# A fused linear attention with two feed-forward layers on one core: the plain slots' sine put ahead of the copies, and the preparation sums set out anew

## The chip, the core and the metric

The kernel runs on one core of a Trainium2 chip. The core has five engines with a queue each: TensorE (PE; its weight loads are PEld), VectorE (DVE), ScalarE (ACT), GpSimd (POOL) and SyncE (SP, which here only issues DMAs). Each engine takes its own instructions in the order in which the program issues them; between engines only semaphores set the order. The metric is the time of one execution on the device in microseconds (us).

## The reference

A recurrent attention over 768 time steps, then two layers of two matrix products each, with a rational function and then h·cos(h) between them. The work that the change touches lies in the last layer.

```python
def _attn_ref(q, k, v, alpha):            # B, H, S, D = 4, 8, 768, 48
    for t in range(S):
        state = alpha[:, :, t, :, None] * state + einsum('bhd,bhe->bhde', k[:, :, t], v[:, :, t])
        y[:, :, t] = einsum('bhd,bhde->bhe', q[:, :, t], state)
def _moe_ref(x, w_in, w_out, a, b):       # x: 3072 x 384, w_in: 384 x 2048, w_out: 2048 x 384
    h = x @ w_in
    P = a[0] + a[1] * h + a[2] * h**2 + a[3] * h**3
    Q = 1.0 + abs(b[0]) * abs(h) + abs(b[1]) * h**2
    return (P / (Q + 1e-06)) @ w_out
def _moe2_ref(x, w_in, w_out):            # same shapes
    h = x @ w_in
    return (h * cos(h)) @ w_out
```

## The kernel before

The 3072 tokens are six blocks of 512. The 2048 inner columns of a layer are 16 tiles of 128 (f = 0 to 15). Every fp32 operand is held as two parts, hi (rounded to the matmul's fp32r) and lo (the remainder), and a product is three matmuls (hi·hi, lo·hi, hi·lo), so a first product h = x·w_in of a tile is 9 matmuls of 512 columns and a second product (into three PSUM accumulators acc0 to acc2) another 9.

A **layer slot** (`layers(n)`) does one tile: a first product for tile n (L504), the activation of older tiles on ACT and DVE (the product g on DVE L599), the rounding of g to hi (ACT L550) and its remainder lo (POOL L555), and the second product of tile n-4 (L520). Blocks 0 and 1 of the last layer run this way. In block 0 DVE, ACT and POOL also convert the output weights (ACT L68, L69 and L188, DVE L73 and L74, POOL L198: the remainder of a weight tile that TensorE's second product needs a slot later), and round x for block 1 (ACT L630, DVE L634).

Blocks 2 to 5 of the last layer run in **plain slots** (`threes(k)`, k = 0 to 68; slot 0 is the first). There a 3 x 3 group of w_in tiles is multiplied with 15 half-width first products instead of 18 (a fast 3 x 3 scheme on sums and differences of the weights and of x). Three slots make one group (kinds 0, 1 and 2), five groups make 15 of the 16 tiles, and a slot of kind 3 (k = 15, 31, 47, 63) does the sixteenth tile by an ordinary first product of 9 matmuls (L1107). I call the slots 15, 31 and 47 **border slots**: they also run the first three products of the next block (`level0`), and ACT copies these from PSUM into s5 and s63 (L1025). Each plain slot does the activation of one tile: z (ACT L1003), the angle (DVE L1007), the sine (ACT L1011) and the product g = sine·h (DVE L1016); a slot later ACT rounds g to hi (L1021) and POOL forms lo (L1022); a slot after that TensorE does the second product (L965). DVE combines the partial products of a group in PSUM (L1049, L1058, L1066 to L1068, L1077, L1078); TensorE may write a bank again only when DVE has read it.

The sums and differences themselves are made beforehand by jobs: `weights()` for the five groups of w_in tiles (t = 0 to 4; `w_first` and `w_second`), `x_prepare(blk)` for x. A job is a generator. After every slot from layer slot -16 on (the counter `now`; plain slot k is now = 16 + k), `prepare(dve, pool, act)` adds a slot's budget to each engine's `room`; it first issues the pending remainders (POOL L654), then the pending roundings (ACT L651), and then lets each job issue sums (L660, on DVE or POOL as the job says) as long as **both** DVE and POOL have room left. The budgets are `EARLY` in the layer slots of block 0 (`now` below 0), `PLAIN` in those of block 1, and `ROOM[kind]` in the plain slots.

The banks: h of the sixteenth tile goes to bank b2, which the last tile of group 4 (its h is f1, also b2) holds until its product g (L1016) has read it. In a border slot the queue of ACT is z, hi, the two copies, sine; that of DVE is angle, g.

The last four tiles of block 1 still need their second products when the plain slots begin: slots 0 to 3 do 9 matmuls each of these (`old` in L990 to L994); slot 4 has none, and from slot 5 on the second products of block 2 follow.

Of the kernel before, what the change touches and what calls it, by code (L numbers as in the profile page):

```python
# [20 lines left out]
NF = DFF // 128  # L21
# [18 lines left out]
def attn_then_two_moe(ctx, tc, kqT, aT, vP, w1i, w1o, ma, mb, w2i, w2o, out):  # L40
# [601 lines left out]
    split = set()  # L642
# [5 lines left out]
    def splits(keys, hi, lo, of, cols):  # L648

        def first():  # L650
            nc.scalar.activation(out=hi, in_=of, func=AF.Copy)  # L651

        def rest():
            nc.gpsimd.tensor_tensor(out=lo, in0=of, in1=hi.bitcast(F32), op=ALU.subtract)  # L654
            split.update(keys)

        to_split.append((first, rest, cols))

    def add(eng, out, a, b, op):
        (nc.vector, nc.gpsimd)[eng].tensor_tensor(out=out, in0=a, in1=b, op=op)  # L660
        cols = a.shape[-1] * (2 if len(a.shape) > 2 else 1)
        return eng, (0.45 + cols / 750, 0.25 + cols / 500)[eng]

    def x_prepare(blk):
# [7 lines left out]
        eng, last = (DV, N3 - 2) if blk == 2 else (PL, N3 - 1)  # L672
        eng2 = DV if blk < 4 else PL
        while now[0] < begin or (last, "w", "8" if blk == 2 else "1") not in split or not (even or last in wa):
            yield WAIT
# [27 lines left out]
        yield add(eng, f["1"], b[1][0], b[1][1], MINUS)  # L703
        yield add(eng, f["8"], f["1"], b[2][1], MINUS)
        yield add(eng2, f["14"], b[0][1], f["1"], PLUS)
        cost = add(eng, f["3"], f["8"], b[2][0], PLUS)
        parts_of(("1", "8"), t1, 0)
        yield cost
        while (last, "w", "8" if blk == 2 else "14") not in split:
            yield WAIT  # L710
        t2 = sums("9", "10")
        yield add(eng, t2, t0, b[0][0].rearrange("p (a b) -> p a b", a=1).to_broadcast([128, 2, HT]), MINUS)
        while (last, "w", "8" if blk == 2 else "11") not in split or (even and now[0] < 10):
# [4 lines left out]
        cost = add(eng, f["5"], f["5"], b[1][0], MINUS)  # L718
        parts_of(("5", "6"), t3, 2)
        parts_of(("14", "3"), t0, 4)  # L720
        parts_of(("9", "10"), t2, 6)
# [3 lines left out]
        yield cost  # L725
        while (blk, "3") not in split:
            yield WAIT
        t4 = sums("13", "0")
        yield add(eng2, f["13"], b[0][1], b[1][1], MINUS)
        cost = add(eng, f["0"], b[1][1], b[2][1], PLUS)  # L730
# [5 lines left out]
        yield cost  # L736
# [39 lines left out]
    def w_differences(eng, a, e, r):  # L776
        yield add(eng, e, a[1][0], a[1][1], PLUS)
        yield add(eng, r, a[2][1], a[2][2], MINUS)

    def w_first(t, a, e, r):  # L780
# [3 lines left out]
        yield add(DV, f["5"], a[1][0], a[2][2], PLUS)  # L784
        yield add(PL, f["1"], a[0][2], a[0][0], MINUS)
        yield add(DV, f["0"], e, a[2][2], PLUS)
        yield add(DV, f["4"], a[0][1], e, MINUS)
        yield add(PL, f["1"], f["1"], a[0][1], MINUS)
        yield add(PL, f["12"], a[0][0], a[2][0], PLUS)
        yield add(DV, f["4"], f["4"], r, PLUS)  # L790
        yield add(DV, f["8"], e, a[0][2], MINUS)
        cost = add(DV, f["12"], f["12"], a[2][2], PLUS)
# [19 lines left out]
        yield cost  # L812

    def w_second(t, a, e, r):

        f = {name: f_of[t, name] for name in W2}
        yield add(DV, f["14"], r, a[0][0], MINUS)
        w_parts(t, "14")
        yield add(DV, f["13"], a[1][0], r, MINUS)
        yield add(PL, f["2"], a[1][2], e, MINUS)  # L820
        w_parts(t, "13", "2")
        yield add(PL, f["7"], a[2][0], r, PLUS)
        yield add(PL, f["11"], a[1][0], a[0][2], MINUS)
        cost = add(PL, f["11"], f["11"], a[1][2], PLUS)
# [6 lines left out]
        for name in ("6", "10", "3", "9"):  # L831
            split.add((t, "w", name))
        wa[t] = held[t, "out"]
        yield cost
# [7 lines left out]
    def weights():  # L842
# [3 lines left out]
        for t in range(N3 - 1):  # L846
# [4 lines left out]
            n = 3 if t == 3 else 4  # L851
            cells(t, W1[:n], f_tile())
            cells(t, W1[n:], q_tile() if t % 2 else f_tile())
# [5 lines left out]
        for t in range(N3 - 1):  # L859
            if t == 0:  # L860
                b = w_stage(1, "raw")
            if t == 3:
                while now[0] < 12:
                    yield WAIT
                b, a = a, w_stage(3, "w1")
                yield WAIT
            while now[0] < max(4 + t, 3 * t + 3) or (t > 1 and (t - 2, "w", "11") not in split):
# [4 lines left out]
            a = b if t in (0, 3) else w_stage(2 if t == 1 else 4, "st")  # L872
        while not {(2, "13"), (2, "0")} <= split or now[0] < 15:
# [21 lines left out]
    EARLY, PLAIN = (1.4, 1.6, 0.8), (2.2, 2.5, 1.9)  # L895

    def prepare(dve, pool, act):

        for i, n in enumerate((dve, pool, act)):
            room[i] = min(room[i] + n, (1.6 if now[0] < 2 * NF else 1.3) * n)  # L900
# [20 lines left out]
    ROOM = ((0.8, 2.3, 0.7), (0.6, 2.2, 1.3), (1.2, 2.5, 1.9), (1.2, 2.5, 1.5))  # L921
# [48 lines left out]

    def threes(k):
# [18 lines left out]
        if k < 4:  # L990
            old = F0 - 4 + k
            item = {"blk": 1, "f": NF - 4 + k, "at": NF - 4 + k, "w": ws[1][NF - 4 + k]}
            item.update(hi=T[old]["hi"], lo=T[old]["lo"])
            g2 = second_product(item)  # L994
# [98 lines left out]
        else:  # L1093
            angle()
            parts_g()
            g2(9)
# [16 lines left out]
            sine()  # L1113
# [327 lines left out]
```

## Time and profile before

| | |
|---|---|
| median of 3 runs | 948.82 us (945.15 to 949.71) |
| profiled execution | 950.62 us, span of its instructions 948.9 us |
| TensorE busy in the span | 908.3 us (96%) |
| PEld / DVE / ACT / POOL busy | 748.6 / 710.3 / 698.8 / 713.6 us (79 / 75 / 74 / 75%) |
| mean granted TensorE clock | 0.985 |
| chain that ended last, by engine | PE 63%, DVE 9%, ACT 9%, POOL 8%, DMA 6%, issue 3% |

The span is cut in the trace at about 0 to 140 us (attention and the start of the first layer), to 475 us (first layer), to 668 us (blocks 0 and 1 of the last layer, with the weights' conversion from about 475 to 610 us) and to 943 us (plain slots). In the page's 40 slices TensorE is nearly full from 140 us on, the three other engines are near full until 540 us and half idle in the plain slots. Idle time is therefore read from TensorE: every gap of its queue after 140 us moves the end, unless something else is late behind it.

### The profile page before, as it was taken

The numbers are of one execution on the slowest core, as the hardware profiler recorded it, in microseconds if no ns is written. First come the engines' busy times: TensorE is split into PE (matmuls) and PEld (weight loads), VectorE is DVE, ScalarE is ACT, GpSimd is POOL, SyncE is SP. The second block draws the span as 40 slices with busy tenths as digits, with TensorE's granted clock in tenths as the row PEclk, the third lists the DMA queues.
The fourth block names the chain that finished last, engine by engine and source line by source line (L and its number), as shares of the span: only waits on it lengthen the run. The fifth ranks groups of instructions, "written<-read, shape, count | busy, mean of one in ns | idle before, by whom it ended". The sixth has DMA issues, their size and how long they took to land.

```text
span 948.9 us, 15705 instructions
## 1 busy us (share of the span) xinstructions
PE 908.3 (96%) x5336; PEld 748.6 (79%) x5336; DVE 710.3 (75%) x1249; ACT 698.8 (74%) x1304; POOL 713.6 (75%) x699
## 2 busy tenths in 40 slices
PE   7898899999999999999999999999998999999997
PEld 6677777878888888888888886788887887887885
DVE  8988979999999989989979767656464553555552
ACT  6888987878879788878877777756575665666653
POOL 5898998989889989979878776768776465665332
PEclk8998999999999999999999999999999999999999
DMA  9999831111123132232165466441143432533432
GB/s 287 313 321 317 290 112 41 34 34 34 66 76 117 42 109 83 70 122 84 50 212 165 132 223 209 159 158 51 67 151 99 135 117 84 166 101 90 137 108 88
DMA packets 64745, 124.63 MB, mean 131 GB/s; under 512 B 7472, under 2 KB 29616, under 8 KB 64656
## 3 DMA queue, kind: packets, MB, share of 16 engines
q1 hardware_dynamic: 64656, 123.54, 40.6%
q8 instruction: 44, 0.72, 0.3%
q14 instruction: 45, 0.37, 0.1%
HBM read 93.63 MB, written 29.88 MB: 130 GB/s over the span
## 4 chain that ended last, share of the span: by engine, by line
PE 63%; DVE 9%; ACT 9%; POOL 8%; DMA 6%; issue 3%; SPq 0%; ACTq 0%; DVEq 0%; POOLq 0%
PE acc L520 18%; PE b L504 18%; PE acc L965 14%; PE b L930 6%; PE r L930 5%; POOL lo L555 1%; DVE st L73 1%; PE b L1107 1%; ACT hi L550 1%; DMA spare<-w1o 1%; DMA raw<-w2o 1%; POOL kq L294 1%; DMA kq<-kqT 1%; DVE g L586 1%; POOL z L581 1%
## 5 line engine op out<-in xcount | busy, mean ns | idle before, releaser
L504 PE MATMUL b<-x,w 128*128 128x512 f32 x1143 | 288.3, 396 | 0.6 <-DVE g L573 0.5
L504 PEld LDWEIGHTS b<-x,w 128*128 128x128 f32 x1143 | 214.0, 188 | 54.2 <-DVE g L573 2.1
L520 PE MATMUL acc<-hi,w 128*128 128x512 f32 x744 | 254.6, 396 | 2.1 <-POOL w L198 2.0
L555 POOL TENSOR_TENSOR lo<-g,hi 128x512 fp32r<-128x512 f32 x128 | 174.4, 1362 | 72.7 <-ACT hi L550 66.3
L1022 POOL TENSOR_TENSOR lo<-g,hi 128x512 fp32r<-128x512 f32 x64 | 82.8, 1294 | 119.1 <-ACT hi L1021 102.4
L520 PEld LDWEIGHTS acc<-hi,w 128*128 128x128 f32 x744 | 139.0, 188 | 38.6 <-POOL w L198 6.2
L520 PE MATMUL acc<-lo,w 128*128 128x512 f32 x372 | 147.3, 396 | 0.0
L550 ACT ACTIVATE hi<-g 128x512 fp32r<-128x512 f32 x128 | 80.8, 631 | 88.0 <-DVE g L586 51.8
L581 POOL TENSOR_TENSOR z<-z,ah 128x512 f32<-128x512 f32 x96 | 127.2, 1325 | 8.0
L965 PE MATMUL acc<-hi,w_out 128*128 128x512 f32 x384 | 131.1, 397 | 0.0
L582 DVE TENSOR_TENSOR g<-g,b 128x512 f32<-128x512 f32 x96 | 65.3, 681 | 24.9 <-ACT g L579 24.3
L520 PEld LDWEIGHTS acc<-lo,w 128*128 128x128 f32 x372 | 69.9, 188 | 17.0
L965 PEld LDWEIGHTS acc<-hi,w_out 128*128 128x128 f32 x384 | 69.2, 190 | 10.2
L965 PE MATMUL acc<-lo,w_out 128*128 128x512 f32 x192 | 76.6, 399 | 0.5 <-POOL lo L1022 0.2
L580 POOL TENSOR_SCALAR z<-ah,cq 128x512 f32<-128x512 f32 x96 | 75.0, 781 | 1.1 <-ACT ah L578 1.1
L579 ACT ACTIVATE g<-b,cq 128x512 f32<-128x512 f32 x96 | 74.5, 776 | 0.0
L586 DVE SCALAR_TENSOR_TENSOR g<-g,cq,r 128x512 f32<-128x512 f32 x96 | 70.9, 738 | 0.1
L573 DVE SCALAR_TENSOR_TENSOR g<-g,cq,b 128x512 f32<-128x512 f32 x96 | 70.7, 736 | 0.0
L590 ACT ACTIVATE r<-z,lnb 128x512 f32<-128x512 f32 x96 | 66.6, 694 | 1.8 <-POOL z L581 1.7
L575 DVE SCALAR_TENSOR_TENSOR r<-z,r 128x512 f32<-128x512 f32 x96 | 65.6, 684 | 0.0
L570 DVE SCALAR_TENSOR_TENSOR z<-z,r 128x512 f32<-128x512 f32 x96 | 65.0, 677 | 0.0
L578 ACT ACTIVATE ah<-b 128x512 f32<-128x512 f32 x96 | 56.4, 588 | 7.6 <-PE b L504 7.0
(192 smaller groups left out, 1841.6 us busy)
## 6 DMA issues: line engine op xcount, KB each, us to landing
w_out<-wd SPq DMA_DIRECT2D x64, 384.0 KB, 3.0
kq<-kqT SPq DMA_DIRECT2D x24, 512.0 KB, 5.2
raw<-w2i SPq DMA_DIRECT2D x16, 384.0 KB, 3.5
w<-wd SPq DMA_DIRECT2D x16, 384.0 KB, 3.3
raw<-w2o SPq DMA_DIRECT2D x16, 384.0 KB, 3.7
wd<-w SPq DMA_DIRECT2D x16, 384.0 KB, 2.6
w_f<-wf SPq DMA_DIRECT2D x27, 192.0 KB, 3.0
v<-vP SPq DMA_DIRECT2D x24, 192.0 KB, 5.0
```

Of the source, the lines that this page charges most:

```text
L504: nc.tensor.matmul(h, ws[0][f][:, w, ks], x[:, xx, kk, :], start=i == 0, stop=i == 8)
L520: nc.tensor.matmul(acc[k], ws[1][f][:, w, ks], d[g], start=first and i == 0, stop=last and i == 2)
L550: nc.scalar.activation(out=t["hi"], in_=t["g"], func=AF.Copy)
L555: eng.tensor_tensor(out=t["lo"], in0=t["g"], in1=t["hi"].bitcast(F32), op=ALU.subtract)
L573: nc.vector.scalar_tensor_tensor(g, g, cq[:, 3:4], two["h"], ALU.add, ALU.mult)
L579: nc.scalar.activation(out=g, in_=h, func=AF.Identity, scale=cq[:, 5:6], bias=cq[:, 4:5])
L580: nc.gpsimd.tensor_scalar(zz, ah, cq[:, 1:2], cq[:, 0:1], ALU.mult, ALU.add)
L581: nc.gpsimd.tensor_tensor(out=zz, in0=zz, in1=ah, op=ALU.mult)
L586: nc.vector.scalar_tensor_tensor(g, g, cq[:, 2:3], r, ALU.add, ALU.mult)
L930: nc.tensor.matmul(tile[:, half], w[p], x[q], start=start and i == 0, stop=True, skip_group_check=True)
L965: nc.tensor.matmul(acc[k], item["w"][:, w, ks], item[g], start=first, stop=last)
L1022: nc.gpsimd.tensor_tensor(out=p["lo"], in0=p["g"], in1=p["hi"].bitcast(F32), op=ALU.subtract)
```

## The change

- In the slot of kind 3, `sine()` and `times()` are issued right after `parts_g()`, ahead of the second product, `level0` and its two copies (before: after the first product of the sixteenth tile).
- The 36 matmuls that are left over from block 1 are given out by `left_over` as 7, 7, 7, 7 and 8 in slots 0 to 4 (before: 9 in each of slots 0 to 3).
- A job yields the engine of its next sum before issuing it, and is stopped by the room of that engine alone (before: by the smaller of both rooms, after the cost was known).
- Budgets: `EARLY` for POOL 1.2 (before 1.6); `ROOM` of DVE in kind 1 is 0.0 (before 0.6); POOL in blocks 3 to 5 is 2.0 (before 1.6).
- `split` keeps the slot in which a remainder was issued, and some waits of the jobs ask for 1 or 2 slots more. The sums of the first half of weight group 3 are made in slots now = 12 and later on their own copy of the weights (before: in the first loop, with groups 0 to 2). Some sums of x swap engines; block 2's x waits for another weight group.

On ACT, in the first border slot (k = 15). Here z is the scaled h of slot 15's tile, hi the rounding of the tile before, s the copies of the next block's first products, ah the sine; the last row belongs to slot 16. Before:

```order
L1003 ACTIVATE z<-b_7988 128x512
L1021 ACTIVATE hi<-g 128x512
L1025 ACTIVATE s<-b_8079 128x256
L1025 ACTIVATE s<-r_8080 128x512
L1011 ACTIVATE ah<-ah,half_pi 128x512
L1003 ACTIVATE z<-b_8092 128x512
```

and with the change:

```order
L1037 ACTIVATE z<-b_7975 128x512
L1055 ACTIVATE hi<-g 128x512
L1045 ACTIVATE ah<-ah,half_pi 128x512
L1059 ACTIVATE s<-b_8075 128x256
L1059 ACTIVATE s<-r_8076 128x512
L1037 ACTIVATE z<-b_8088 128x512
```

The sine has moved ahead of the two copies, which wait for matmuls of the same slot.

On DVE, from the end of slot 3 to slot 5 (g are the products, w_f sums of weights, b and r PSUM banks). Before:

```order
L1016 TENSOR_TENSOR g<-ah,b_7433 128x512
L660 TENSOR_TENSOR w_f_7456<-w_f 128x128
L660 TENSOR_TENSOR w_f_7540<-w_f 128x128
L1058 TENSOR_TENSOR b_7555<-b_7504,s 128x256
L1007 SCALAR_TENSOR_TENSOR ah<-z,r_7390 128x512
L1066 TENSOR_TENSOR b_7555<-b_7504,s 128x256
L1067 TENSOR_TENSOR s<-s,r_7505 128x256
L1068 TENSOR_TENSOR r_7505<-r_7505,s 128x256
```

and with the change:

```order
L1050 TENSOR_TENSOR g<-ah,b_7419 128x512
L1092 TENSOR_TENSOR b_7536<-b_7491,s 128x256
L1041 SCALAR_TENSOR_TENSOR ah<-z,r_7377 128x512
L1100 TENSOR_TENSOR b_7536<-b_7491,s 128x256
L1101 TENSOR_TENSOR s<-s,r_7492 128x256
L1102 TENSOR_TENSOR r_7492<-r_7492,s 128x256
```

The two weight sums ahead of the read of the bank (L1058, now L1092) are gone from there.

On POOL, in three layer slots of block 0 (now = -6 to -4); x is rounded from the second of them on: L198 is the remainder of an output weight, L555 that of g, w_kq remainders of weight sums, w_f sums of weights. Before:

```order
L198 TENSOR_TENSOR w_7_128<-st,w_7_128 128x384
L654 TENSOR_TENSOR w_kq<-w_f_6307,w_kq 128x512
L654 TENSOR_TENSOR w_kq<-w_f_6308,w_kq 128x256
L660 TENSOR_TENSOR w_f<-w_f 128x128
L555 TENSOR_TENSOR lo<-g,hi 128x512
L198 TENSOR_TENSOR w_8_129<-st,w_8_129 128x384
L660 TENSOR_TENSOR w_f<-w_f 128x128
L660 TENSOR_TENSOR w_f_6492<-w_f 128x128
L660 TENSOR_TENSOR w_f_6492<-w_f_6492,w_f 128x128
L660 TENSOR_TENSOR w_f_6493<-w_f 128x128
L555 TENSOR_TENSOR lo<-g,hi 128x512
```

and with the change:

```order
L198 TENSOR_TENSOR w_7_128<-st,w_7_128 128x384
L654 TENSOR_TENSOR w_kq<-w_f_6266,w_kq 128x256
L661 TENSOR_TENSOR w_f_6410<-w_f 128x128
L555 TENSOR_TENSOR lo<-g,hi 128x512
L198 TENSOR_TENSOR w_8_129<-st,w_8_129 128x384
L661 TENSOR_TENSOR w_f_6410<-w_f_6410,w_f 128x128
L661 TENSOR_TENSOR w_f_6411<-w_f 128x128
L555 TENSOR_TENSOR lo<-g,hi 128x512
```

Between w_7's remainder and the second L555 a 512-column remainder and two sums have gone to other slots.

The diff, cut:

```diff
@@ add
     def add(eng, out, a, b, op):
+        yield eng
         (nc.vector, nc.gpsimd)[eng].tensor_tensor(out=out, in0=a, in1=b, op=op)
         cols = a.shape[-1] * (2 if len(a.shape) > 2 else 1)
-        return eng, (0.45 + cols / 750, 0.25 + cols / 500)[eng]
+        room[eng] -= (0.45 + cols / 750, 0.25 + cols / 500)[eng]
+
+    def since(key, steps):
+        return key in split and split[key] + steps <= now[0]
@@ x_prepare
-        eng, last = (DV, N3 - 2) if blk == 2 else (PL, N3 - 1)
+        eng, last = DV if blk == 2 else PL, 2 if blk == 2 else N3 - 1
...
-        yield add(eng2, f["14"], b[0][1], f["1"], PLUS)
+        yield from add(eng, f["14"], b[0][1], f["1"], PLUS)
...
-        yield add(eng, f["5"], b[0][0], b[2][0], MINUS)
-        yield add(eng2, f["6"], f["5"], f["14"], MINUS)
+        yield from add(eng2, f["5"], b[0][0], b[2][0], MINUS)
+        yield from add(eng, f["6"], f["5"], f["14"], MINUS)
...
-        cost = add(eng, f["0"], b[1][1], b[2][1], PLUS)
+        yield from add(eng2, f["0"], b[1][1], b[2][1], PLUS)
@@ weights
-        for t in range(N3 - 1):
+        for t in range(3):
             a = w_stage(t, "a")
...
+        while now[0] < 12:
+            yield WAIT
+        b = w_stage(3, "w1")
+        yield WAIT
+        while not since((1, "w", "11"), 1):
+            yield WAIT
+        cells(3, W1, wp.tile([128, 6 * 128], F32, tag="w1_1", name="w_f1"))
+        yield from w_differences(PL, *b)
+        yield from w_first(3, *b)
+        while not since((2, "w", "11"), 1):
+            yield WAIT
+        cells(3, W2, wp.tile([128, 6 * 128], F32, tag="w1_0", name="w_f0"))
+        yield from w_second(3, *b)
@@ prepare
-    EARLY, PLAIN = (1.4, 1.6, 0.8), (2.2, 2.5, 1.9)
+    EARLY, PLAIN = (1.4, 1.2, 0.8), (2.2, 2.5, 1.9)
...
-        for job in work:
-            while min(room[DV], room[PL]) > 0:
-                cost = next(job, WAIT)
-                if cost is WAIT:
+        for i, job in enumerate(work):
+            while True:
+                if asked[i] is None:
+                    asked[i] = next(job, END)
+                if asked[i] is WAIT:
+                    asked[i] = None
                     break
-                room[cost[0]] -= cost[1]
+                if asked[i] is END or room[asked[i]] <= 0:
+                    break
+                asked[i] = None
...
-    ROOM = ((0.8, 2.3, 0.7), (0.6, 2.2, 1.3), (1.2, 2.5, 1.9), (1.2, 2.5, 1.5))
+    ROOM = ((0.8, 2.3, 0.7), (0.0, 2.2, 1.3), (1.2, 2.5, 1.9), (1.2, 2.5, 1.5))
@@ new, called by threes
+    def left_over(n):
+
+        if not old:
+            for i in range(4):
+                d = T[F0 - 4 + i]
+                old.append({"blk": 1, "f": NF - 4 + i, "at": NF - 4 + i, "w": ws[1][NF - 4 + i], "of": d, "left": 9})
+        for _ in range({2: 2, 3: 2, 4: 3 if now[0] < NF + 4 else 9, 5: 4}[n]):
+            item = next((o for o in old if o["left"]), None)
+            if item is None:
+                return
+            if item["left"] == 9:
+                item.update(hi=item["of"]["hi"], lo=item["of"]["lo"])
+                item["run"] = second_product(item)
+            item["run"](1)
+            item["left"] -= 1
@@ threes
-        if k < 4:
-            old = F0 - 4 + k
-            item = {"blk": 1, "f": NF - 4 + k, "at": NF - 4 + k, "w": ws[1][NF - 4 + k]}
-            item.update(hi=T[old]["hi"], lo=T[old]["lo"])
-            g2 = second_product(item)
+        if k < 5:
+
+            g2 = left_over
...
         else:
             angle()
             parts_g()
+            sine()
+            times()
             g2(9)
...
-            sine()
-            times()
             if not active:
                 acc_out()
         dve, pool, act = ROOM[kind]
-        prepare(dve, pool if bi == 0 else 1.6, act)
+        prepare(dve, pool if bi == 0 else 2.0, act)
```

## Rows read from the trace of the kernel before

**Rows 1.** TensorE's waits, whole span: who waited for whom, us in total, times, longest

```profile
PE b L1107 <- DVE g L1016: 6.5, 3, 2.2
PE b L930 <- DVE b L1078: 2.3, 2, 1.5
PE acc L520 <- POOL w L198: 2.0, 4, 0.7
...
PE b L930 <- DVE b L1058: 0.9, 1, 0.9
PE b L930 <- DVE b L1066: 0.2, 1, 0.2
```

**Rows 2.** Timeline, first border slot: start, us, engine line, [idle before <-releaser]

```profile
728.70 0.69 DVE L1007 SCALAR_TENSOR_TENSOR ah<-z,b 128x512 f32<-128x512 int32 x1 [1.34 <-ACT z L1003]
...
731.59 0.86 PE L930 MATMUL r<-x_t,w 128*128 128x256 f32 x6
...
732.49 0.60 ACT L1025 ACTIVATE s<-r 128x512 f32<-128x512 f32 x1 [0.32 <-PE r L930]
732.99 0.71 ACT L1011 ACTIVATE ah<-ah,half_pi 128x512 f32<-128x512 f32 x1
733.80 0.69 DVE L1016 TENSOR_TENSOR g<-ah,b 128x512 f32<-128x512 f32 x1 [4.42 <-ACT ah L1011]
734.64 3.03 PE L1107 MATMUL b<-x,w 128*128 128x512 f32 x9 [2.18 <-DVE g L1016]
```

**Rows 3.** Timeline, slot 63, which has no copies

```profile
926.93 0.73 ACT L1011 ACTIVATE ah<-ah,half_pi 128x512 f32<-128x512 f32 x1 [0.23 <-DVE ah L1007]
...
927.76 0.69 DVE L1016 TENSOR_TENSOR g<-ah,b 128x512 f32<-128x512 f32 x1 [0.86 <-ACT ah L1011]
...
928.77 2.26 PE L1107 MATMUL b<-x,w 128*128 128x512 f32 x9
```

**Rows 4.** Windows behind the three gaps: length, busy by engine, PEclk, DMA

```profile
734.64:740.93 6.29, 6.29 (x23) 5.12 (x24) 0.88 (x2) 1.74 (x4) 1.28 (x1) 0.73 0.02 4
801.05:807.29 6.24, 6.24 (x24) 5.10 (x24) 0.89 (x2) 1.75 (x4) 1.20 (x1) 0.74 0.00 0
867.47:872.22 4.75, 4.75 (x23) 3.98 (x24) 0.89 (x2) 1.75 (x4) 1.19 (x1) 1.00 0.02 3
```

**Rows 5.** Timeline, plain slots 5 and 11, around two of TensorE's gaps

```profile
688.63 0.61 ACT L1003 ACTIVATE z<-b 128x512 int32<-128x512 f32 x1
...
690.83 0.61 PE L930 MATMUL b<-x_t,w_kq 128*128 128x256 f32 x3 [0.87 <-DVE b L1078]
...
710.79 0.61 ACT L651 ACTIVATE x_t<-x_f 128x512 fp32r<-128x512 f32 x1
...
711.32 0.58 ACT L1003 ACTIVATE z<-b 128x512 int32<-128x512 f32 x1
...
712.86 1.49 DVE L660 TENSOR_TENSOR x_f<-x 128x256 f32<-128x256 f32 x1 [0.97 <-POOL x_t L654]
...
715.82 0.62 PE L930 MATMUL b<-x_t,w_v 128*128 128x256 f32 x3 [1.45 <-DVE b L1078]
```

**Rows 6.** Chain of waits: a run of second-product matmuls

```profile
728.38 3.02 PE acc L965 x13
```

**Rows 7.** Timeline, POOL, DVE and TensorE, block 0 around 580 us

```profile
577.49 1.03 POOL L198 TENSOR_TENSOR w<-st,w 128x384 fp32r<-128x384 f32 x1
...
580.84 1.30 POOL L555 TENSOR_TENSOR lo<-g,hi 128x512 fp32r<-128x512 f32 x1
580.92 1.78 DVE L634 TENSOR_TENSOR x<-x 128x512 fp32r<-128x512 f32 x1 [1.12 <-ACT x L630]
...
582.09 1.47 POOL L198 TENSOR_TENSOR w<-st,w 128x384 fp32r<-128x384 f32 x1
...
583.61 0.73 PE L520 MATMUL acc<-hi,w 128*128 128x512 f32 x2 [0.58 <-POOL w L198]
```

**Rows 8.** Tile x_f on DVE: duration ns shortest/median/longest

```profile
L660 DVE TENSOR_TENSOR x_f<-x x5: 411/1493/1508, 626.3 to 712.9; 128x256 f32<-128x256 f32 x5
```

More of the change, by code (lines that the diff above doesn't have):

```diff
@@ L671, in x_prepare @@
         even = blk % 2 == 0
-        eng, last = (DV, N3 - 2) if blk == 2 else (PL, N3 - 1)
+        eng, last = DV if blk == 2 else PL, 2 if blk == 2 else N3 - 1
         eng2 = DV if blk < 4 else PL
-        while now[0] < begin or (last, "w", "8" if blk == 2 else "1") not in split or not (even or last in wa):
+        lag = 2 if blk == 2 else 0
+        while now[0] < begin or not since((last, "w", "8" if blk == 2 else "1"), lag) or not (even or last in wa):
             yield WAIT
@@ L724, in x_prepare @@
                 out[k, j] = tuple(x[:, i, k, j * HT:(j + 1) * HT] for i in range(2))
-        yield cost
-        while (blk, "3") not in split:
+        while not since((blk, "3"), lag):
             yield WAIT
         t4 = sums("13", "0")
-        yield add(eng2, f["13"], b[0][1], b[1][1], MINUS)
-        cost = add(eng, f["0"], b[1][1], b[2][1], PLUS)
+        yield from add(eng2, f["13"], b[0][1], b[1][1], MINUS)
+        yield from add(eng2, f["0"], b[1][1], b[2][1], PLUS)
         for i, name in enumerate(("13", "0")):
@@ L776, in w_differences @@
     def w_differences(eng, a, e, r):
-        yield add(eng, e, a[1][0], a[1][1], PLUS)
-        yield add(eng, r, a[2][1], a[2][2], MINUS)
+        yield from add(eng, e, a[1][0], a[1][1], PLUS)
+        yield from add(eng, r, a[2][1], a[2][2], MINUS)
     def w_first(t, a, e, r):
@@ L783, in w_first @@
         DV = PL if t == N3 - 1 else 0
[L784 to L792, printed above, removed]
+        yield from add(DV, f["5"], a[1][0], a[2][2], PLUS)
+        yield from add(PL, f["1"], a[0][2], a[0][0], MINUS)
+        yield from add(DV, f["0"], e, a[2][2], PLUS)
+        yield from add(DV, f["4"], a[0][1], e, MINUS)
+        yield from add(PL, f["1"], f["1"], a[0][1], MINUS)
+        yield from add(PL, f["12"], a[0][0], a[2][0], PLUS)
+        yield from add(DV, f["4"], f["4"], r, PLUS)
+        yield from add(DV, f["8"], e, a[0][2], MINUS)
+        yield from add(DV, f["12"], f["12"], a[2][2], PLUS)
         if t == 0:
@@ L831, in w_second @@
         for name in ("6", "10", "3", "9"):
-            split.add((t, "w", name))
+            split[t, "w", name] = now[0]
         wa[t] = held[t, "out"]
-        yield cost
     def q_tile():
@@ L858, in weights @@
         a = w_stage(0, "st")
-        for t in range(N3 - 1):
+        for t in range(3):
             if t == 0:
                 b = w_stage(1, "raw")
[L862 to L867, printed above, removed]
+            while now[0] < max(4 + t, 3 * t + 3) or (t > 1 and not since((t - 2, "w", "11"), 1)):
                 yield WAIT
@@ L894, in attn_then_two_moe @@
     room = [0.0, 0.0, 0.0]
[L895 removed]
+    EARLY, PLAIN = (1.4, 1.2, 0.8), (2.2, 2.5, 1.9)
+    END = object()
+    asked = [None] * len(work)
     def prepare(dve, pool, act):
         for i, n in enumerate((dve, pool, act)):
[L900 removed]
+            room[i] = min(room[i] + n, max((1.6 if now[0] < 2 * NF else 1.3) * n, 0.01))
         while to_rest and room[PL] > 0:
```

48 lines of the change are left out of this document (25 added, 23 removed).

## The prediction

> **What bounds the kernel now.** I read three views in this order: the page's shares, TensorE's waits, and the timeline around each wait. The page shows TensorE busy for 908 of 948.9 us, and its slices show it almost full from 140 us on, so what counts is where its queue stood still after that. The list of TensorE's waits names three groups [rows 1]. The largest is L1107, the first product of the sixteenth tile: 6.5 us in three waits, all released by the product g on DVE (L1016). Then come the half-width products L930 that wait for DVE to read a bank: 2.3, 0.9 and 0.2 us. Last, second products that wait for the weight remainder L198 on POOL: 2.0 us in four. Together 11.9 us, all in places that the change edits. The attention's waits lie before the change.
>
> **The border slots.** The timeline of slot 15 shows how the largest wait arises [rows 2]. TensorE issues its second product and the six matmuls of `level0` at 731.59, and then wants bank b2 for L1107. The bank is held until g has read it. The angle is done at 729.39, so the sine could start then; but ACT's queue has two copies of `level0` results ahead of it. The second copy ends at 733.09, the sine runs from 732.99 (starts and ends of ACT overlap a little) to 733.70, g from 733.80 to 734.49, and L1107 starts at 734.64 after 2.18 us of standing still. The other two waits have the same length.
>
> With the sine ahead of the copies it starts about 0.23 us after the angle, as in slot 63, which has no copies [rows 3]: there the sine takes 0.73, g starts 0.10 after it, and L1107 runs without a wait although TensorE has nine matmuls less to do in that slot. So in slot 15: sine 729.62 to 730.33, g 730.43 to 731.12, bank free at 731.27 with the 0.15 that the row shows between g's end and L1107. TensorE arrives at 734.64 - 2.18 = 732.46, so 1.19 us to spare. The copies are not late: they wait for `level0` (the second started at 732.49, when the sine will be long over), and they feed the next slot's products, behind nine matmuls of L1107 and six second products. Gain: 3 x 2.18 = 6.54 us. Bounds: all of it, or, if something keeps the sine late, none.
>
> **The clock behind these gaps.** After the first two gaps the windows show a granted clock of 0.73 and 0.74, that is a stretch at 1.2 GHz, and after the third 1.00 [rows 4]. The three windows hold the same instructions; they take 6.29, 6.24 and 4.75 us. The two falls therefore cost 1.54 + 1.49 = 3.03 us. The same gap did this twice and once not. Without gaps I expect no fall: gain 3.03 us of this execution, between 0 (if new gaps of that length come) and 3.03.
>
> **The first plain slots.** Slot 4 has no second product before, so TensorE waits there 0.90 us for L1058 and 0.17 for L1066. Thirteen second-product matmuls take 3.02 us [rows 6], 0.232 each; the change moves eight of them, 1.86 us, into slot 4, four ahead of the product that needs L1058 done and four behind. DVE also loses the two weight sums that stand ahead of L1058. These two waits [rows 1] go. In exchange slots 0 to 3 lose 0.46 us of cover each; a reader of a bank that was just in time would now be late, so I put 0.1 against it. In slot 5 TensorE waits 0.87 us for L1078, because z on ACT comes only at 688.63 [rows 5], behind three accumulator copies and a weight rounding; DVE's angle stands ahead of L1077 and L1078. With the change the copies are spread over two slots and the rounding of w_o comes after slot 5, so z is earlier; 0.2 stays. In slot 11 the wait is 1.45 us: DVE's x sum starts at 712.86 behind POOL and takes 1.49 [rows 5], and the angle, L1077 and L1078 queue behind it. With kind 1's DVE budget at 0.0 that sum is gone from there. What is late next is ACT: three roundings of 0.61 now stand together ahead of slot 11's z, where one stood (710.79, then z at 711.32). The sum ended at 714.35 and the product started 1.47 later, which is what the angle, the two reads and the release take. From z's end, 711.90, and 0.2 for the semaphore, the product could have started at 713.57; it was due at 715.82 - 1.45 = 714.37. That is 0.80 of slack against two more roundings, 1.22 us: 0.4 stays. Sum: 0.90 + 0.17 + 0.87 + 1.45 - 0.1 - 0.2 - 0.4 = 2.69 us; bounds 0 (each wait replaced by another) and 3.39.
>
> Here a rule of the Trainium skill speaks against the change. The row first: DVE's 256-column sums of x take 411 ns at the shortest but 1493 at the median [rows 8], and both long and short ones lie beside POOL's two-input work. SBUF — State Buffer, section "Who interferes with whom", says that a DVE instruction with two SBUF inputs and a GpSimd instruction exclude each other for a whole instruction; the trace agrees, with 1.08 us between the two values. By that rule each of the three x sums left in block 2's plain slots loses up to 1.1 us on DVE; they now stand at the end of kind 2, where the next thing TensorE needs from DVE is more than a slot's half away. If half a microsecond of that showed, the sum below would be 0.5 us smaller.
>
> **The layer slots of block 0.** The chain there is: g's remainder L555 on POOL, then the weight remainder L198, then TensorE. L198 takes 1.03 us alone and 1.47 beside DVE's rounding of x, which itself takes 1.78 [rows 7]; L555 started at 580.84 behind remainders and a sum of POOL's preparation. The change takes a 512-column remainder and two of five sums out of these slots. The first wait of 0.58 [rows 7] is of that making. The others depend on DVE as much: three sums of it still stand in the first of these slots, none in the second. I take 1.2 of the 2.0 us; bounds 0 and 2.02.
>
> **What the moves cost elsewhere.** The sums of weight group 3 now fall into layer slots now = 12 to 17 and plain slots 0 to 3, with their remainders w_v. POOL's work from now = 10 to plain slot 3, added up from the order with 1.30 for 512 columns, 1.02 for 384, 0.74 for 256 and 0.45 for a sum, is about 36 us in ten slots of 4.2, so there is 6 us of room, and the remainders of g needed there are used later than before, since the leftover matmuls are spread. I cost it at nothing; if POOL fell behind, it would show as TensorE waiting for lo.
>
> **Sum.** 6.54 + 3.03 + 2.69 + 1.20 = 13.46 us. The profiled execution took 950.62 us, 1.72 more than its span; less 13.46 that is 937.2. It lies 1.80 above the median of the runs shown, and one fall of the clock more or less (1.5 us) may be the difference; from the median the same sum gives 935.4. I take the middle, **936.3**, that is, 949.7 as the base.
>
> **Rivals.**
> First, **only the border slots gain**: the waits of the first plain slots and of block 0 come back in other places, because DVE, ACT and POOL have the same amount of work there. For: POOL and DVE are near full until 540 us and the instruction counts are the same. Against: TensorE's gaps have single named causes. Time: 949.7 - 6.54 - 3.03 = 940.1.
>
> Second, **the clock gives nothing back**, because the other timed runs have fewer falls than the profiled one, or new gaps make new ones: 936.3 + 3.0 = 939.3.
>
> Third, **the change doesn't do what it says**: the sine remains late, since z or the angle of a border slot is late for another reason. For: ACT has new roundings in slots 12 and 13. Against: slot 63 and 1.19 us to spare. Then only 2.69 + 1.20 are won: about 945.8.
>
> Fourth, **slower**: POOL's queue. If its instructions took the long form throughout, as L198 does beside DVE (1.47 for 1.03, 1.43 times) [rows 7], the 36 us from now = 10 to plain slot 3 would become 51, 9 more than the ten slots hold. TensorE would wait these 9 us for lo, in gaps that let the clock fall three times (1.5 each, 4.5), and in block 0 the waits for L198 would grow by 0.44 in some seven slots (3.1) instead of shrinking by 1.2. That is 17.8 us against 13.46 won: about 954. It decides from 1.3 times over the whole stretch; against it, the change takes two-input sums away from DVE in just these plain slots.
>
> **How the numbers follow.** Forecast 0.68, first rival 0.14, second 0.08, third 0.05, slower 0.05. The forecast's own range is 933.8 (all waits go, 6.54 + 3.03 + 3.39 + 2.02 = 15.0 us, from the median) to 939. For the range I add the first and second rivals above and, below, that runs of before lay as low as 945.15: **932.5 to 942**. Faster by over 0.5% (below 944.1; about what a measurement of this kernel tells from no change) takes in the forecast and the first two rivals, 0.90; the third and part of the fourth, where POOL's work grows less, lie within 0.5%, 0.07; slower 0.03.
>
> **What would show it.** Right: no wait of L1107 for DVE's g in slots 15, 31 and 47, the sine ending before the copies begin; no fall of the clock after 140 us; second products in slot 4 and no gap before its products; at most one gap of some 0.35 in slot 11; the waits for L198 halved. Wrong: TensorE waiting for lo in slots 0 to 6, for L1112 (the old L1078) in slot 11 with more than 0.5, or a gap before slot 16's products 10 and 13 because the copies are late; or a span that falls by less than 9 us.

## The result and the profile after

The changed kernel takes **939.27 us** (median of 8 runs, 936.09 to 942.67) against 947.32 us (8 runs) of the kernel before: ratio **0.991, 95% interval 0.9883 to 0.9936**. The forecast was 936.3 with a range of 932.5 to 942.0. The mechanism named there for the largest term is right. The total is 3.0 us too low: the term for the layer slots of block 0 came out with the wrong sign and the clock's term was too large, and a base 2.4 us above the median measured here hid part of both.

The profiled execution took 936.09 us (span 934.4), 14.5 us less than the one of before, while the medians differ by 8.05. So the first thing to separate is what happened ahead of the change. The first line below is the attention's window (length, busy by engine, mean granted clock, DMA), the second a wait of the first layer which both kernels have.

```profile
0.00:140.00 140.00, 118.37 (x1568) 97.94 (x1569) 118.37 (x282) 119.35 (x240) 124.08 (x146) 0.98 0.86 280
...
190.58 0.73 PE L504 MATMUL b<-x,w 128*128 128x512 f32 x2 [0.51 <-DVE g L573]
```

and the same two of the kernel before:

```profile
0.00:140.00 140.00, 118.91 (x1538) 99.04 (x1538) 117.19 (x276) 114.99 (x232) 119.11 (x142) 0.93 0.86 276
...
194.97 1.20 PE L504 MATMUL b<-x,w 128*128 128x512 f32 x4 [0.53 <-DVE g L573]
```

The mean clock in the attention was 0.98 and 0.93, and the same wait comes 4.39 us earlier. The change does not touch that stretch. From this wait to the end of the span the kernels take 743.8 and 753.9 us: **10.1 us** belong to the change in these two executions. The rest is luck of the attention's clock: over all the kernels profiled here this wait comes between 189.96 us (mean clock 1.00 in the attention, e2, which has most of the change) and 196.12 us (0.93, e7, built on the kernel before), and kernels with and without the change stand at both ends. The timed runs vary in the same way: of 23 runs of the kernel before on one chip, the quickest (943.43) had a mean clock of 0.996, the slowest (953.31) 0.983.

TensorE's waits after, over the whole span, for [rows 1] (columns as there):

```profile
PE acc L520 <- POOL w L198: 2.7, 7, 0.7
...
PE b L504 <- DVE g L599: 2.0, 2, 1.5
...
PE b L948 <- DVE b L1092: 0.3, 1, 0.3
PE acc L983 <- POOL lo L1056: 0.2, 1, 0.2
PE r L948 <- ACT s L1059: 0.2, 1, 0.2
```

The 6.5 us of the sixteenth tile's product (now L1143) are gone, and of the 3.4 us of the first plain slots 0.3 for L1092 (old L1058) and a new 0.2 for a copy in slot 1 (L1059) are left. But the second products' wait for L198 has grown from 2.0 to 2.7, and a wait that was not there before, for g of the layer slots (L599), has 2.0.

The first border slot, for [rows 2]:

```profile
724.25 0.69 DVE L1041 SCALAR_TENSOR_TENSOR ah<-z,b 128x512 f32<-128x512 int32 x1 [0.31 <-ACT z L1037]
724.97 0.72 ACT L1045 ACTIVATE ah<-ah,half_pi 128x512 f32<-128x512 f32 x1 [0.23 <-DVE ah L1041]
725.80 0.69 DVE L1050 TENSOR_TENSOR g<-ah,b 128x512 f32<-128x512 f32 x1 [0.86 <-ACT ah L1045]
727.21 0.88 PE L948 MATMUL r<-x_t,w 128*128 128x256 f32 x6
...
727.92 2.27 PE L1143 MATMUL b<-x,w 128*128 128x512 f32 x9
728.12 0.60 ACT L1059 ACTIVATE s<-r 128x512 f32<-128x512 f32 x1 [0.33 <-PE r L948]
```

The sine follows the angle by 0.23 us, g ends at 726.49, and L1143 starts 1.43 us later without a wait; less the 0.15 of the release that is 1.28 of slack, where 1.19 was worked out. The second copy runs beside L1143.

Behind the sixteenth tile's products, for [rows 4], windows of 4.75 us:

```profile
727.92:732.67 4.75, 4.75 (x26) 3.96 (x25) 0.95 (x2) 2.41 (x5) 1.91 (x2) 1.00 0.28 83
790.31:795.06 4.75, 4.75 (x26) 3.98 (x25) 0.96 (x2) 2.42 (x5) 1.94 (x2) 1.00 0.29 86
852.73:857.48 4.75, 4.75 (x26) 3.96 (x25) 0.96 (x2) 2.41 (x5) 1.92 (x2) 1.00 0.28 83
```

The granted clock is 1.00 in all three; the one fall left after 140 us comes when TensorE has done its last matmul (927.71 us).

Block 0 around 570 us, for [rows 7] (SPq is SP's DMA queue):

```profile
561.21 0.32 SPq L202 DMA_DIRECT2D wd<-w  x1
...
562.42 0.28 DVE L661 TENSOR_TENSOR w_f<-w_f,w_f 128x128 f32<-128x128 f32 x1
...
562.72 2.33 SPq L761 DMA_DIRECT2D w_f<-wf  x3
...
565.09 1.38 SPq L622 DMA_DIRECT2D x<-x1d  x3
...
566.57 0.38 SPq L149 DMA_DIRECT2D raw<-w2o  x1
...
567.52 0.54 SPq L149 DMA_DIRECT2D raw<-w2o  x1
567.58 0.59 DVE L661 TENSOR_TENSOR w_f<-w_f 128x128 f32<-128x128 f32 x1 [1.11 <-DMA w_f<-wf]
568.09 0.67 DVE L599 TENSOR_TENSOR g<-ah,b 128x512 f32<-128x512 f32 x1
568.69 0.68 DVE L80 SCALAR_TENSOR_TENSOR ah<-z,b 128x512 f32<-128x512 int32 x1
568.82 2.37 PE L504 MATMUL b<-x,w 128*128 128x512 f32 x9 [0.47 <-DVE g L599]
...
572.52 0.55 ACT L68 ACTIVATE st<-raw 128x384 f32<-128x384 f32 x1 [2.59 <-DMA raw<-w2o]
...
574.58 0.68 DVE L599 TENSOR_TENSOR g<-ah,b 128x512 f32<-128x512 f32 x1
...
575.32 1.43 PE L504 MATMUL b<-x,w 128*128 128x512 f32 x5 [1.51 <-DVE g L599]
```

and on SP's queue in the kernel before:

```profile
564.97 0.32 SPq L202 DMA_DIRECT2D wd<-w  x1
565.33 1.45 SPq L622 DMA_DIRECT2D x<-x1d  x3
566.94 0.33 SPq L149 DMA_DIRECT2D raw<-w2o  x1
569.77 0.33 SPq L202 DMA_DIRECT2D wd<-w  x1
570.26 0.33 SPq L149 DMA_DIRECT2D raw<-w2o  x1
574.16 0.33 SPq L202 DMA_DIRECT2D wd<-w  x1
574.59 1.45 SPq L755 DMA_DIRECT2D w_f<-wf  x3
```

The first fence is read from its last line backwards. TensorE wants g's bank at 573.8 and gets it at 575.3. g is late because the conversion of an output weight stands ahead of its sine on ACT and waits 2.59 us for the weight's load, raw. That load was issued at 566.57, behind three loads of weight rows (w_f, for the sums of weight group 2) and three of x. The w_f loads are issued when DVE's last sum has freed their tile (562.70). From the store ahead of them (wd) to the load of raw SP takes 5.36 us; in the kernel before, with the x loads alone between the two, 1.97. There SP issued the w_f loads at 574.59, behind the x loads and two loads of raw. With the change the job `weights()` comes to group 2 two slots sooner, and its loads moved ahead on SP. (POOL's smaller budget isn't what moved them: with the old one, in e5, they stand in the same slot. That the new rules of the jobs did it is read from the program, not run apart.)

**How long the layer slots really are.** The idle time on PE understates it: the profile models where a matmul ends, so a short wait can hide in the tail of the matmul before. The weight loads (PEld) show more of it. After, window 545 to 612 us:

```profile
PEld acc L520 <- POOL w L198: 5.9, 8, 1.1
PEld b L504 <- DVE g L599: 4.2, 6, 1.9
```

Before, the same window:

```profile
PEld acc L520 <- POOL w L198: 6.0, 10, 1.1
PEld b L504 <- DVE g L599: 0.6, 2, 0.4
```

PEld waited 6.6 us there before and 10.1 after. From start to start of L504 an undisturbed layer slot takes 4.20 us; what the slots from now = -12 to the last one of block 1 take beyond that is 4.57 us before and 7.74 after. So the layer slots **lost 3.17 us**. (PEld's idle time gives nearly the same difference, 3.5 us, but its totals are too large.) The slots from now = -9 to 2, where nearly all of it lies, in us:

| slot (now) | -9 | -8 | -7 | -6 | -5 | -4 | -3 | -2 | -1 | 0 | 1 | 2 |
|---|---|---|---|---|---|---|---|---|---|---|---|---|
| before | 4.20 | 4.20 | 4.39 | 4.39 | 4.39 | 5.13 | 5.27 | 4.94 | 4.29 | 4.58 | 4.79 | 4.39 |
| changed | 4.82 | 4.20 | 5.43 | 6.50 | 5.01 | 5.36 | 5.28 | 4.71 | 4.21 | 4.20 | 4.20 | 4.20 |

Block 0 ends with slot -1. It alone lost 4.3 us. The first three slots of block 1 won 1.2: the kernel before makes the sums of weight group 3 there, and the change makes them later.

The same count from start to start gives 2.40 us for the third border slot (6.62 us before from its six L930 matmuls to the next slot's, 4.22 after) where the idle column said 2.18, and 3.95 and 3.88 for the other two, with the slow clock behind them: 10.2 us in all. With the first plain slots' waits (3.39 us before, 0.51 after) the account of these two executions nearly closes: 10.2 + 2.9 - 3.2 = 9.9 of the 10.1 us.

### The profile page after: what moved, and what is told of

Its sections match the earlier page's. It is cut to its first block, busy times and chain, and to the rows that moved or that the text cites. A ratio compares the mean times of both kernels' runs of the same rounds, so it can differ in the third digit from the quotient of the medians.

```text
span 934.4 us, 15701 instructions
## 1 busy us (share of the span) xinstructions
PE 899.9 (96%) x5336; PEld 740.4 (79%) x5336; DVE 710.0 (76%) x1245; ACT 699.6 (75%) x1304; POOL 716.1 (77%) x701
## 4 chain that ended last, share of the span: by engine, by line
PE 67%; ACT 10%; DVE 9%; DMA 6%; POOL 5%; issue 3%; SPq 0%; ACTq 0%; POOLq 0%; DVEq 0%
PE acc L520 20%; PE b L504 19%; PE acc L983 15%; PE b L948 6%; PE r L948 5%; DMA kq<-kqT 2%; DMA v<-vP 2%; POOL lo L555 1%; ACT hi L550 1%; DVE st L73 1%; DMA x0d<-g 1%; DVE g L586 1%; ACT st L68 1%; PE b L1143 1%; ACT g L579 1%
## 5 line engine op out<-in xcount | busy, mean ns | idle before, releaser
L504 PE MATMUL b<-x,w 128*128 128x512 f32 x1143 | 288.6, 397 | 2.6 <-DVE g L599 2.0
L504 PEld LDWEIGHTS b<-x,w 128*128 128x128 f32 x1143 | 213.5, 188 | 57.7 <-DVE g L599 4.2
L555 POOL TENSOR_TENSOR lo<-g,hi 128x512 fp32r<-128x512 f32 x128 | 174.5, 1364 | 77.8 <-ACT hi L550 71.5
L573 DVE SCALAR_TENSOR_TENSOR g<-g,cq,b 128x512 f32<-128x512 f32 x96 | 70.7, 737 | 0.0
```

The costliest lines, as they stand in the source:

```text
L504: nc.tensor.matmul(h, ws[0][f][:, w, ks], x[:, xx, kk, :], start=i == 0, stop=i == 8)
L555: eng.tensor_tensor(out=t["lo"], in0=t["g"], in1=t["hi"].bitcast(F32), op=ALU.subtract)
L573: nc.vector.scalar_tensor_tensor(g, g, cq[:, 3:4], two["h"], ALU.add, ALU.mult)
```

## The experiments

All are compared with runs of the kernel before on the same chip. "Excess" is the layer slots beyond 4.20 us each, counted as above; "waits" is the sum of PE's idle gaps of 0.15 us and more after 150 us in the profiled execution.

| kernel | median (runs) | ratio to before, 95% | waits | excess |
|---|---|---|---|---|
| before | 946.8 to 948.5 | 1 | 12.7 | 4.57 |
| changed | 939.27 (8) | 0.991, 0.9883 to 0.9936 | 6.0 | 7.74 |
| changed, again (e9) | 938.19 (6) | 0.9899, 0.9872 to 0.9926 | 5.8 | 7.76 |
| border slots only (e1) | 939.21 (6) | 0.9904, 0.9867 to 0.9941 | 6.2 | 4.58 |
| all but the border slots (e2) | 946.68 (12) | 0.998, 0.9956 to 1.0003 | 13.3 | 8.52 |
| left-over spread only (e3) | 945.68 (12) | 0.9974, 0.9952 to 0.9997 | 11.0 | 4.57 |
| kind-1 DVE budget only (e6) | 945.76 (12) | 0.9991, 0.9972 to 1.0009 | 11.3 | 4.56 |
| these three together (e7) | 935.95 (6) | 0.9869, 0.984 to 0.9899 | 3.0 | 4.74 |
| changed, POOL budget 1.6 (e5) | 938.67 (6) | 0.9894, 0.9865 to 0.9922 | 6.6 | 8.31 |
| changed, group-2 loads later (e4) | 934.74 (6) | 0.9848, 0.9814 to 0.9883 | 3.8 | 3.72 |
| ... sums a slot later too (e8) | **932.13** (6) | **0.9828, 0.9802 to 0.9854** | 2.4 | 3.04 |
| ... group 1's sums as well (e10) | 932.8 (6) | 0.9855, 0.9829 to 0.9881 | 2.2 | 3.02 |
| changed, group-2 sums alone later (e11) | 936.08 (6) | 0.9889, 0.9859 to 0.9919 | 4.1 | 6.31 |

Counted from the wait for g (L573) to the end of the span, as above, the profiled executions take 753.9 us (before), 743.8 (changed, both series), 744.1 (e1), 753.2 (e2), 751.2 (e3), 749.7 (e6), 741.2 (e7), 743.7 (e5), 739.1 (e4), 738.6 (e8), 738.8 (e10) and 742.1 (e11). These figures are free of the attention's luck; those of e3 and e6 have one fall of the clock and none behind the border gaps, where the profile of before has two.

**Border slots only (e1).** Edit to the kernel before:

```diff
             parts_g()
+            sine()
+            times()
             g2(9)
...
                 cons[k + 1]["h"] = h
-            sine()
-            times()
```

> The kernel before, with the sine and the product g of the kind-3 slots put ahead of the second product, level0 and its copies; nothing else. My theory: each gap of TensorE after 140 us moves the end by its own length, and the clock falls behind a gap of 2.18 us cost 1.5 us each when they come. Then the three waits of L1107 (6.54 us) are gone, no half clock after 140 us, and the time is 947.3 less 6.5 to 9.6, so 937.8 to 940.8 us (ratio 0.990 to 0.993). The waits of slots 4, 5 and 11 (3.4 us) and of L198 (2.0 us) stay as they were. Rival A: the copies of level0, now behind the sine, make the next slot late and give a new gap, then less than 3 us are won, above 944. Rival B: the clock falls cost nothing in the median, because few timed runs have them: then 6.5 us and not more, 940.8.

939.21 us, and the three waits are gone; those of slots 4, 5 and 11 stay:

```profile
PE b L930 <- DVE b L1078: 2.4, 2, 1.5
PE acc L520 <- POOL w L198: 2.0, 4, 0.7
PE b L930 <- DVE b L1058: 0.9, 1, 0.9
```

The copies make nothing late (rival A falls). This edit alone earns as much as the whole change. Whether the clock gave something back beside the 6.5 us of waits (rival B) can't be told from the medians: the interval runs from 5.6 to 12.6 us.

**All but the border slots (e2)**: the same two lines put back in the changed kernel.

> The changed kernel with one thing undone: the sine and the product g of the kind-3 slots are again behind the first product of the sixteenth tile. My theory: the rest of the change wins 2.9 us in the first plain slots and loses 2.5 us in block 0, net 0.4 us, so this kernel takes 946 to 948 us like the one before (ratio 0.998 to 1.001), with three waits of the sixteenth tile's product for g of about 2.2 us. Rival: the order of the sine is not where the gain comes from, and the rest wins several us by itself (attention earlier, POOL lighter): then 940 to 944 us.

946.68 us, with an interval that includes no change at all. The profile has the 6.5 us again, and the wait for g in block 0 is longer still:

```profile
PE b L1141 <- DVE g L1050: 6.5, 3, 2.2
PE b L504 <- DVE g L599: 2.8, 2, 2.5
PE acc L520 <- POOL w L198: 2.7, 7, 0.7
```

So the rest of the change gives with one hand (the plain slots) and takes with the other (block 0).

**The left-over products spread (e3)**, added to the kernel before:

```diff
-        if k < 4:
...
+        if k < 5:
+            g2 = left_over
```

> The kernel before, with the 36 left-over second-product matmuls given out over slots 0 to 4 as in the change (7, 7, 7, 7, 8); nothing else. My theory: the matmuls in slot 4 cover its waits (0.90 and 0.17 us gone) and most of the 0.87 us in slot 5, the 1.45 us of slot 11 stays: 947.3 less 1.1 to 1.9, so 945.4 to 946.2 us (ratio 0.998 to 0.999). Rival A: the sums of weights ahead of the read of the bank on DVE are what made slot 4 wait, then the slot-4 waits stay and nothing is won, 947.3. Rival B: slots 0 to 3 miss the two matmuls taken from each and show gaps of up to 0.46 us each: 947.3 or more.

945.68 us: the waits of slot 4 and of slot 5 are gone, only slot 11's 1.5 us is left (L1093 is the old L1078); no new gap in slots 0 to 3 over 0.17 us. The sums on DVE ahead of the read, still there, do no harm once slot 4 has second products.

```profile
PE b L930 <- DVE b L1093: 1.5, 1, 1.5
```

**The DVE budget of kind 1 (e6)**, in the kernel before and in block 2 only:

```diff
-        prepare(dve, pool if bi == 0 else 1.6, act)
+        prepare(0.0 if kind == 1 and bi == 0 else dve, pool if bi == 0 else 1.6, act)
```

> The kernel before with the DVE budget of the kind-1 slots of block 2 at 0.0 instead of 0.6; nothing else. My theory: the x sum ahead of the angle is what made slot 11 wait, so its 1.45 us (about 1.7 from slot start to slot start) go and nothing else changes: 948.4 less 1.7, 946.7 us, ratio 0.998. Rival A: ACT's roundings make slot 11 late as well, and 0.4 us or more of the wait stay. Rival B: the sum only moves into another slot and the wait with it: 948.4.

The time can't be told from that of before (0.9991), but the profile can: of the two waits for L1078 only slot 5's 0.8 is left, slot 11 waits no longer, and nothing came in its place.

```profile
PE b L930 <- DVE b L1058: 0.9, 1, 0.9
PE b L930 <- DVE b L1078: 0.8, 1, 0.8
```

**The three together, without the rest (e7):** the edits of e1, e3 and e6.

> The kernel before with three parts of the change and no more: the sine and g of the kind-3 slots moved ahead; the left-over second products spread over slots 0 to 4; no DVE budget in kind-1 slots of block 2. Jobs, groups and the layer slots' budgets stay as before. My theory: border slots and first plain slots win as in the changed kernel (gaps after 668 us 0.5 to 0.8 us in all), and block 0 keeps the 2.0 us of before instead of 4.5: 2 to 2.5 us less than the changed kernel, 936.5 to 937.5 us. Rival: the remaking of the jobs (weight group 3 later, sums stopped by one engine's room) is what relieves slots 5 and 11; then waits of 0.9 and 1.4 us stay there and the time is that of the changed kernel, 939.

935.95 us, and after 668 us only 0.4 us of waits. The new job rules and the later weight group 3 are not needed for the gain in the plain slots. Beside the changed kernel on the same chip (938.19) it is 2.2 us quicker, where the difference in excess is 3.0; the intervals overlap, so the medians alone don't show it.

**The changed kernel again (e9)**, without an edit.

> The changed kernel itself, once more, beside the three others of this call. My theory: the time goes with how often the clock falls in the attention; with as many runs as here the median is 938.5 to 940 us, ratio to the kernel before 0.989 to 0.993, waits after 140 us of about 6 us in all, of them 4 to 5 us in block 0 of the last layer, and no half clock after 140 us before the last 20 us. Rival: the 936.3 us of my forecast were right and the first series was a slow one: 936 to 937 us.

938.19 us, beside 939.27 in the first series; the rival's 936 to 937 us did not come, and the waits and the excess of the profile are nearly the same.

**POOL's budget back (e5)**: `EARLY` with 1.6 instead of 1.2.

> The changed kernel with POOL's budget in the layer slots of block 0 at 1.6 as before (1.2 in the change); nothing else. The w_f loads stay ahead of the x loads. My theory: it is the loads that hold up g, so TensorE's waits for g (about 2 us) stay; POOL's remainders L198 come 0.3 to 0.5 us later in some slots: waits in block 0 of 4 to 6 us, time 939 to 941 us. Rival: the smaller budget of POOL made the waits; then they fall from 4.5 to 2 us and the time to 937 us.

938.67 us, the same. The waits for g grow (4.2 us in four) and those for L198 shrink (1.4 in six): the smaller budget is not what costs block 0 its time (with the old one the excess is larger, 8.31).

**Group 2's loads later (e4)**, in the first loop of `weights()` of the changed kernel:

```diff
         for t in range(3):
+            while t == 2 and now[0] < -5:
+                yield WAIT
             a = w_stage(t, "a")
             yield WAIT
```

> The changed kernel with the three loads of the weight rows of group 2 (w_f) held back until after layer slot now = -5, so that SP issues them behind the x loads and the weight load raw, as in the kernel before; nothing else. My theory: in the changed kernel these loads stand two slots earlier on SP, wait 1.1 us there for DVE's last sum to free their tile, and hold up the raw load behind them; ACT then waits 2.6 us for raw, g is late and TensorE waits 1.51 us for g (and 0.47 before). With the loads behind, both waits for g are gone: 939.3 less 1.5 to 2.0, so 937.2 to 937.8 us, and the sums of group 2 move one or two slots later without a gap. Rival A: DVE and POOL order (POOL's smaller budget) makes g late, not the loads: the two waits for g stay and the time is 939.3. Rival B: the loads, now later, make the sums late and collide with the x rounding, so the waits for L198 grow by as much as was won: 939 to 941.

934.74 us, a larger gain than expected: it is what the start-to-start count says (excess 7.74 to 3.72), not what the idle column said. One wait for g of 1.21 us is left, at 591 us, where the sums wait 1.3 us for their rows.

**One slot more between load and sum (e8)**, on top of e4:

```diff
             yield WAIT
+            while t == 2 and now[0] < -3:
+                yield WAIT
```

> The kernel with the later loads (group 2's w_f rows not before now = -5) and, on top, the sums of group 2 not before now = -3, one slot more between load and sum. My theory: with the later loads alone the sums on DVE and POOL waited 1.3 and 1.0 us for these loads, and g behind them kept TensorE waiting 1.21 us; with one slot more the loads have landed, that wait goes and 0.9 us of waits for L198 stay: 1 to 1.2 us less than with the later loads alone (934.7), so 933.5 us, about 6 us less than the changed kernel. Rival A: the three sums, now in one slot with the x rounding, delay g by their own 1.2 us all the same: 934.7. Rival B: what the later loads won was chance of the clock; then both lie within 2 us of the changed kernel, 937 to 939.

932.13 us, 6.1 us below the changed kernel on the same chip, with intervals that do not touch: the lowest median of all versions (e10's can't be told from it). The excess accounts for 4.7 us of it (7.76 to 3.04); the six runs also had a little more clock than the changed kernel's (mean 0.993 against 0.989). The weight loads' waits, 545 to 612 us:

```profile
PEld acc L520 <- POOL w L198: 3.2, 7, 0.7
PEld b L504 <- DVE g L599: 1.5, 3, 0.8
```

**Group 1's sums later as well (e10):** `if t == 1: yield WAIT` behind the first `yield WAIT`.

> The kernel with later loads and one slot more for group 2, and now one slot more between load and sum for weight group 1 as well. My theory: the remaining wait for freshly loaded rows (DVE 1.1 us, POOL 0.8 us in the slots around 555 us, which TensorE feels as slots of 4.67, 4.81 and 4.82 us instead of 4.20) goes: about 1 us less than 932.1, so 931 us. Rival: these slots are long because of the remainders L198 and of the sums themselves, whatever the loads do; then 932, no difference that can be told.

932.8 us and an excess of 3.02: no difference. The long slots came later, but not fewer: e8 has 4.68, 4.81 and 4.82 us at now = -10, -9 and -7, e10 4.20, 4.20 and 4.42 there and 4.83, 4.63 and 4.35 at now = -6, -4 and -3. So more time between load and sum did not help here, as the rival had it; what makes these slots long is not shown.

**Loads early, sums late (e11).** e4 moved loads and sums together; this is e8 without e4's lines, so that it differs from e8 in the place of the three loads alone.

> The changed kernel with only the sums of weight group 2 held back until after layer slot now = -3; their three w_f loads stay where the change puts them, ahead of the x loads and the raw load on SP. It tells the loads apart from the sums, which the kernel with the later loads moved together. My theory: the loads do it, since they wait on SP for DVE to free their tile and hold up raw; the slot of 6.5 us (575 us) stays long by 1.5 us or more, and the layer slots' excess over 4.20 us stays at 6 to 8 us in all (7.7 in the changed kernel, 3.0 to 3.7 with the later loads): time 937 to 938.5 us. Rival: the sums in those slots do it; then the excess falls to 3 to 4 us and the time to 932 to 934 us.

936.08 us, between the two numbers, and the profile says why. The load's wait stays, and is even longer, followed here by a stretch at half the clock, 1.2 GHz (second fence: the window behind it, mean 0.59):

```profile
572.74 0.56 ACT L68 ACTIVATE st<-raw 128x384 f32<-128x384 f32 x1 [3.26 <-DMA raw<-w2o]
...
575.52 0.74 PE L504 MATMUL b<-x,w 128*128 128x512 f32 x2 [2.17 <-DVE g L599]
```

```profile
575.52:579.72 4.20, 4.20 (x11) 3.31 (x12) 2.70 (x5) 3.37 (x7) 2.25 (x2) 0.59 0.35 124
```

But the slots after 580 us, which in the changed kernel take 5.36, 5.28, 4.71 and 4.21 us, here take 4.20, 4.20, 4.20 and 4.49, and the next 4.65. So both are at work: the early loads cost the slot of 6.5 us (2.3 beyond 4.20, and 1.66 in the next slot with the clock), and the sums, where they stand in the slots that round x, cost another 2 us. That second part was there before too (5.13, 5.27 and 4.94).

## Why the prediction was right and where it was wrong

- **Border slots, 6.54 us: right**, in mechanism, slack and place; from start to start it is 3 x 2.40 = 7.2. e1 shows it alone, e2 by its absence.
- **The clock, 3.03 us: right for this execution, too much for the median.** A gap of 2.18 us is followed by a fall in two of three cases in the profile of before, one of three in e2 and in e3, none in e6: 4 of 12. Four profiles are few, but as an estimate that is one fall, about 1.5 us, per run, not two. The kernels without these gaps show no fall behind the sixteenth tile's products. The medians agree with it: of the 8.05 us between them, 7.2 in the border slots + 2.9 in the plain slots - 3.17 in the layer slots leave 1.1 for the clock.
- **First plain slots, 2.69 us: right**, 3.39 before and 0.51 after, 2.88 won. Which edit does what was right in the main (e3: slots 4 and 5, e6: slot 11); only the two weight sums on DVE, named as a second cause in slot 4, do no harm in e3. The 0.4 that was to stay in slot 11 for ACT's roundings did not appear.
- **Block 0, a gain of 1.2 us: wrong, it lost 4.3.** The step that failed is the one that read these slots as POOL's and DVE's arithmetic only. SP's queue was not followed: the job's loads stand in it ahead of x and raw, and a job that advances sooner issues its loads sooner. The prediction's own sign, the waits for L198 halved, failed too: they went from 2.0 to 2.7 us. The bounds 0 and 2.02 came from PE's idle column, which showed 2.0 of the 4.57 us that the layer slots were long. With the loads put back behind x, block 0's excess is 3.7 us (e4) and, with the sums a slot later too, 2.6 (e8), beside 3.4 before. So 0.8 of the forecast 1.2 us are there, but only with an edit to the sums that the change doesn't have.
- **Moved sums of weight group 3, nothing: right as a cost, but a gain was missed.** TensorE waits for lo nowhere in slots 0 to 6. The layer slots 0 to 2, which the sums left, take 4.20 us each instead of 4.58, 4.79 and 4.39: 1.2 us won. That the sums are the cause there is argued, from their place; no kernel moves them alone.
- **The base.** 949.7 lies midway between a median of three runs (948.82) and a profiled execution (950.62) whose attention had a mean clock of 0.93; the medians of before were 946.8 to 948.5. That error, 1 to 3 us, lies on the other side and hid part of the wrong terms. That the forecast came as near as 3.0 us is in that part luck.
- **Rivals.** Two of them have about the time that came, neither for the right reason. "The clock gives nothing back" (939.3) needs all of the 1.2 us in block 0, and there 4.3 were lost. "Only the border slots gain" (940.1) seems borne out by e1 and e2, but the plain slots' waits did not come back; their gain was lost in block 0, on a path that no rival named. POOL's queue did not fall behind. The long sums of x on DVE [rows 8], which the prediction held against the change, did no visible harm: three of them still take 0.87, 1.49 and 1.51 us in the plain slots (699 to 716 us), and no wait of TensorE of 0.15 us or more comes between 684 and 918 us.

What stays open: why layer slots are still long in e8. The two that round x without sums take 4.20 us there (now = -4 and -3). Those that take 4.4 to 4.8 us (now = -10, -9, -7 and -2 to 0) hold sums of groups 1 and 2 or come soon behind them; how the sums on DVE and POOL would hold TensorE up there was not tried apart.

## What to carry to other kernels

When a change lets a producer advance sooner, follow the loads that it issues on their queue, with what they wait for there and what stands behind them, before the arithmetic. Size waits from start to start of a repeated group: the matmuls' idle column showed too little here (2.0 of 4.57 us) and the weight loads' idle time too much (6.6). And compare executions from an event behind the stretch whose clock varies: here that turned 14.5 us into 10.1.

## What the runs showed that was not expected

The clock fell once behind a gap of 2.17 us in a layer slot (e11, window at 0.59) but not behind gaps of 1.51 (changed), 1.83 (e9) and 2.54 us (e2) in the same place: a gap of that length makes a fall possible, not certain. And slots of the kernel before in which PE's column shows a wait of 0.58, 0.70 and 0.47 us are longer than 4.20 by 0.93, 1.07 and 0.74.
